# A token sum moved from ones-matmuls on TensorE to accumulating DMAs in float32

## Chip, cores, metric

One core of one Trainium2 chip. The metric is the device time of one launch in microseconds (us); lower is better.

## The reference, cut to what matters

The program mixes a linear-attention block and an MLP-like block over 2048 tokens of 640 features. Only this part of the attention block matters here:

```python
phi = lambda t: jnp.where(t > 0, t + 1, jnp.exp(t)) + 1e-6
pq, pk = phi(q), phi(k)
kv = jnp.einsum("bhsd,bhse->bhde", pk, v)
z = jnp.einsum("bhsd->bhd", pk)                     # sum of phi(k) over the 2048 tokens
num = jnp.einsum("bhqd,bhde->bhqe", pq, kv)
den = jnp.einsum("bhqd,bhd->bhq", pq, z)[..., None] + 1e-6
o = num / den
```

The change is about how `z`, a vector of 640 sums, is made. It is needed for `den` alone.

## The kernel before

The kernel is a fixed sequence of instructions on each engine (it schedules by hand). In SBUF, tokens lie on 128 partitions in 16 chunks; `pk` is `[128, 16, 640]` in bfloat16. The stages that matter, in order on TensorE: the K stage (to about 32 us) makes `pk`; the Q stage (32 to 74 us) is ten groups, each of ten Q matmuls and five steps of G = x^T pk; then come the `w1_unit`s, with `den_unit`, `kv_unit` and others put between them.

```python
def z_rows():                      # 32 matmuls; sums each 4th chunk into one of 4 column tiles
    p = alloc()
    for (n0, n1) in COLS:          # (0, 512), (512, 640)
        for cc in range(0, NCH, 4):
            for q in range(4):
                mm(PP[p][32 * q:32 * (q + 1), n0:n1], lhsT=ones32[:], rhs=pk[:, cc + q, n0:n1],
                   start=(cc == 0), stop=(cc == NCH - 4), tile_position=(0, 32 * q), ...)
    act(zsb[:], PP[p][:, 0:D], ACT.Copy)
    release(p)
    nc.vector.tensor_copy(zhi[:], zsb[:])
    nc.vector.tensor_tensor(zlo[:], zsb[:], zhi[:], op=ALU.subtract)

def z_cols():                      # 10 matmuls of one column: puts z on partitions
    ...
    for j in range(DC):
        mm(PP[p][:, j:j + 1], lhsT=zh[:, j], rhs=c32[:], start=True, stop=False)
        mm(PP[p][:, j:j + 1], lhsT=zl[:, j], rhs=c32[:], start=False, stop=True)
    nc.vector.tensor_copy(zT[:], PP[p][:, 0:DC])
    for j in range(DC):
        nc.vector.tensor_scalar(Zb[:, j, :], mask32, zT[:, j:j + 1], None, op0=ALU.mult)

# Q stage, ten groups (n_ = 0..9)
    ... # ten Q matmuls, phi, ln1_s (squares on ACT, every 4th also rs1 on POOL), ln1_a (lnxs on DVE,
        # then a transposing DMA lnxT<-lnxs), five g_unit steps
    if n_ == 2:
        z_rows()
    if n_ == 4:
        z_cols()
...
w1_unit(0, 4)        # its gelu goes to shs; then 4 copies of shs on DVE
den_unit()           # needs Zb
rec_piece(0)
w1_unit(0, 0)
kv_unit()
...
```

POOL (GpSimd) computes `rs1`, the layernorm scale of four chunks at a time. `zhi` is z rounded to bfloat16, `zlo` the rest; z_cols multiplies both.

## Time and profile before

| | before |
|---|---|
| time, median of 4 runs | 267.95 us (267.28 to 268.35) |
| span of the profiled run | 266.3 us |
| TensorE (PE) busy | 259.6 us, 97% |
| share of PE in the chain that ended last | 95% |
| z_rows on PE, start to start of the next group | 1.21 us |

The page of the kernel before, its busy times and the engines of the chain that ended last (PEld is the loading of weights into TensorE, DVE is VectorE, ACT ScalarE, POOL GpSimd, SP SyncE; a q marks an engine's sequencer):

```profile
PE 259.6 (97%) x1666; PEld 136.1 (51%) x1699; DVE 116.0 (44%) x212; ACT 110.7 (42%) x165; POOL 32.9 (12%) x111
...
PE 95%; DMA 2%; issue 1%; DVE 0%; SPq 0%
```

PE is busy nearly all the time, and the chain of waits runs through it. Only removing PE time, or making PE wait, can change the total.

The timeline of PE before. Columns: start us, length us, engine, line of the kernel, operation, out<-in, shape, count. L364 is z_rows, L390 the Q matmuls, L423 a w1_unit, L470 den_unit, L443 kv_unit:

```profile
42.99 1.27 PE L364 MATMUL pp<-RPK,ones 128*32 128x512 bf16 x32
44.20 2.35 PE L390 MATMUL pp<-RXT,RA 128*128 128x512 bf16 x9
...
73.59 2.32 PE L423 MATMUL pp<-lnxT,w1x 128*128 128x512 bf16 x10
75.84 1.26 PE L470 MATMUL pp<-pqT,Zb 128*32 128x512 bf16 x20
77.04 2.33 PE L423 MATMUL pp<-lnxT,RB 128*128 128x512 bf16 x9
79.21 1.76 PE L443 MATMUL pp<-RB,RA 128*120 128x120 bf16 x30
```

Read the starts, not the lengths: the 32 matmuls of z_rows run four at a time on column tiles, and from 42.99 to 44.20 they cost 1.21 us. That is the most that removing them can give. PE passes from one stage to the next without a gap.

POOL before, the end of the rs1 work of chunks 4 to 7; the changed kernel starts its DMAs behind it:

```profile
40.61 1.18 POOL L222 TENSOR_TENSOR rs<-ve,nhalf 128x4 f32<-128x4 f32 x1
```

### The profile page before, as it was taken

How to read it: one execution, taken by the hardware profiler on the slowest of the kernel's cores; microseconds unless marked ns; L12 is line 12 of the kernel's file. 1: busy time of each engine (PE TensorE's matmuls, PEld its weight loads, DVE VectorE, ACT ScalarE, POOL GpSimd, SP SyncE). 2: the span in 40 equal slices, each digit the busy share in tenths (PEclk: the TensorE clock that was granted, in tenths of full speed). 3: DMA queues.
4: the chain of work that ended last, by engine and by line, in shares of the span. 5: the costliest groups of instructions: out<-in, count | busy, mean ns of one | idle time of the engine just before them, and what ended most of it. 6: DMA issues, size and time to landing. Idle time of an engine off the chain costs nothing.

```text
span 266.3 us, 4195 instructions
## 1 busy us (share of the span) xinstructions
PE 259.6 (97%) x1666; PEld 136.1 (51%) x1699; DVE 116.0 (44%) x212; ACT 110.7 (42%) x165; POOL 32.9 (12%) x111
## 2 busy tenths in 40 slices
PE   7999999999999999999999999999999999999995
PEld 3555555555545445554444455555544444555552
DVE  2486748665655065999930033233200002233232
ACT  3466663665355771244977522022034444022020
POOL 5000132020200000536870000000000000000000
PEclk9999999999999999999999999999999999999999
DMA  6999993431340269932652001001000000001001
GB/s 204 169 192 301 365 225 68 62 75 25 77 98 0 59 213 362 313 83 49 101 100 49 0 2 49 27 25 49 27 25 0 2 0 0 25 27 49 27 25 49
DMA packets 42245, 23.95 MB, mean 90 GB/s; under 512 B 31090, under 2 KB 41458, under 8 KB 42226
## 3 DMA queue, kind: packets, MB, share of 16 engines
q1 hardware_dynamic: 41474, 22.99, 36.1%
q10 hardware_dynamic: 720, 0.69, 0.8%
q8 instruction: 13, 0.21, 0.3%
q14 instruction: 6, 0.05, 0.1%
q0 software_dynamic: 32, 0.00, 0.0%
HBM read 12.86 MB, written 3.44 MB: 61 GB/s over the span
## 4 chain that ended last, share of the span: by engine, by line
PE 95%; DMA 2%; issue 1%; DVE 0%; SPq 0%
PE pp L638 20%; PE pp L571 19%; PE pp L423 8%; PE pp L597 8%; PE pp L390 8%; PE pp L556 8%; PE pp L261 8%; PE pp L252 8%; DMA RXH<-in_A_x_dram 2%; PE pp L580 2%; PE pp L623 1%; PE pp L632 1%; PE pp L587 1%; PE pp L457 1%; PE pp L443 1%
## 5 line engine op out<-in xcount | busy, mean ns | idle before, releaser
L638 PE MATMUL pp<-RB,RXH 128*128 128x128 bf16 (+1 forms) x381 | 53.5, 297 | 0.7 <-issue 0.3
L571 PE MATMUL pp<-lnxT,RA 128*128 128x512 bf16 x235 | 51.9, 379 | 0.3
L638 PEld LDWEIGHTS <-RXH 128*128 128x128 bf16 x390 | 29.7, 98 | 24.2 <-issue 2.1
L571 PEld LDWEIGHTS <-RA 128*128 128x128 bf16 x240 | 23.4, 98 | 28.0
L600 ACT ACTIVATE RXH<-pp,g_all 128x640 f32<-128x640 f32 x16 | 12.7, 794 | 54.9 <-PE pp L597 54.9
L573 ACT ACTIVATE RXH<-pp 128x1024 bf16<-128x1024 f32 x24 | 24.2, 1019 | 26.7 <-PE pp L571 26.7
L244 ACT ACTIVATE eb<-pp 128x640 bf16<-128x640 f32 (+1 forms) x26 | 21.4, 828 | 25.2 <-PE pp L390 16.3
L261 PE MATMUL pp<-RPK,RXH 128*128 128x128 bf16 (+1 forms) x157 | 25.0, 297 | 0.2
L252 PE MATMUL pp<-RA,RXT 128*128 128x512 bf16 (+1 forms) x157 | 24.0, 300 | 0.2
L390 PE MATMUL pp<-RXT,RA 128*128 128x512 bf16 x97 | 23.1, 379 | 0.2
L597 PE MATMUL pp<-Mp,pqT 128*128 128x512 bf16 (+1 forms) x158 | 23.0, 298 | 0.1
L602 DVE SCALAR_TENSOR_TENSOR RPK<-RPK,omg,RXH 128x640 f32<-128x640 f32 x8 | 7.1, 885 | 36.5 <-ACT RXH L600 36.5
L556 PE MATMUL pp<-w,RXH 128*128 128x128 bf16 (+1 forms) x157 | 21.7, 297 | 0.2
L423 PE MATMUL pp<-lnxT,RB 128*128 128x512 bf16 x77 | 18.1, 379 | 0.2
L261 PEld LDWEIGHTS <-RXH 128*128 128x128 bf16 x160 | 12.7, 98 | 10.4
L247 DVE TENSOR_SCALAR eb<-eb 128x640 bf16<-128x640 bf16 (+1 forms) x26 | 9.5, 365 | 19.3 <-ACT eb L244 19.3
L602 DVE SCALAR_TENSOR_TENSOR RXT<-RXT,omg,RXH 128x640 f32<-128x640 f32 x8 | 7.1, 884 | 24.6 <-ACT RXH L600 24.6
L252 PEld LDWEIGHTS <-RXT 128*128 128x128 bf16 x160 | 12.6, 98 | 9.5 <-DVE RA L329 0.2
L597 PEld LDWEIGHTS <-pqT 128*128 128x128 bf16 x160 | 12.2, 98 | 10.0 <-issue 0.8
L556 PEld LDWEIGHTS <-RXH 128*128 128x128 bf16 x160 | 12.3, 98 | 9.6
L607 DVE SCALAR_TENSOR_TENSOR RXH<-pp,omg,RXT 128x640 bf16<-128x640 f32 x8 | 7.1, 884 | 19.8 <-PE pp L638 19.8
L390 PEld LDWEIGHTS <-RA 128*128 128x128 bf16 x100 | 11.1, 118 | 8.9
(110 smaller groups left out, 238.4 us busy)
## 6 DMA issues: line engine op xcount, KB each, us to landing
out_dram<-RXH SPq DMA_DIRECT2D x15, 160.0 KB, 1.8
RA<-in_B_w_dram SPq DMA_DIRECT2D x5, 432.0 KB, 6.9
RA<-in_A_wqkv_dram SPq DMA_DIRECT2D x2, 800.0 KB, 8.9
RB<-in_B_w_dram SPq DMA_DIRECT2D x1, 1120.0 KB
RXH<-in_A_x_dram SPq DMA_DIRECT2D x2, 480.0 KB, 4.7
RB<-in_B_w_dram SPq DMA_DIRECT2D x1, 960.0 KB, 13.6
RB<-in_B_w_dram SPq DMA_DIRECT2D x1, 800.0 KB, 8.5
Mp<-Mscr SPq DMA_DIRECT2D x1, 800.0 KB
```

Source lines behind the costliest of these rows:

```text
L244: act(e[:, 0:n], src, ACT.Exp)
L252: mm(PP[p][:, n0:n1], lhsT=xT[:, dc, c * P:(c + 1) * P], rhs=wkg[:, dc, n0:n1], start=(dc == 0), stop=(dc == DC - 1))
L261: mm(PP[p][:, n0:n1], lhsT=x_sb[:, c, i * P:(i + 1) * P], rhs=pk[:, c, n0:n1], start=(c == 0), stop=(c == NCH - 1))
L390: mm(PP[p][:, tt * 512:(tt + 1) * 512], lhsT=wqp[:, dc, j], rhs=xT[:, dc, t0:t0 + 512], start=(dc == 0), stop=(dc == DC - 1))
L423: mm(PP[p][:, tt * 512:(tt + 1) * 512], lhsT=lh, rhs=lnxT[:, dc, t0:t0 + 512], start=(dc == 0), stop=(dc == DC - 1))
L556: mm(PP[p][:, n0:n1], lhsT=hsT[:, fc, 2 + c * P:2 + (c + 1) * P], rhs=w2[:, fc, n0:n1], start=(fc == 0), stop=(fc == DC - 1))
L571: mm(PP[p][:, k * 512:(k + 1) * 512], lhsT=w3[:, dc, (fc + k) * P:(fc + k + 1) * P], rhs=lnxT[:, dc, t * 512:(t + 1) * 512], start=(dc == ...
L573: act(h2T[:, t % 2, fc:fc + 2, :], PP[p][:].rearrange("p (k s) -> p k s", k=2), ACT.Gelu_apprx_tanh)
L597: mm(PP[p][:, n0:n1], lhsT=pqT[:, j, c * P:(c + 1) * P], rhs=Mp[:, j, n0:n1], start=(j == 0), stop=(j == DC - 1))
L600: act(ga, PP[p][:, 0:D], ACT.Copy, scale=g_all[:, c:c + 1])
L602: nc.vector.scalar_tensor_tensor(x1(c), x1(c), omg[:, c:c + 1], ga, op0=ALU.mult, op1=ALU.add)
L638: mm(PP[p][:, n0:n1], lhsT=h2T[:, k, fc, cc], rhs=w4[:, fc, n0:n1], start=False, stop=(fc == NF - 1))
```

## The change

The intent: take the 32 ones-matmuls off the busiest engine. Eight DMAs, issued from POOL during the Q stage, add `pk` into a float32 accumulator of `[128, 1280]`, two chunks each; the DMA engines do the adding. Below, one such DMA is a link of the chain, and its landing is the moment when its completion is signalled. TensorE only turns the remaining 128 token rows onto partitions (`z_cols`), now behind `w1_unit(0, 4)`.

```diff
+    RMP = sb("RMP", DC * D)
+    Mp = RMP[:].rearrange("p (j d) -> p j d", j=DC)
+    zacc = RMP[:, 0:4 * D].bitcast(F32)
...
-    def z_rows():            (whole function)
+    def z_add(k):
+        nc.gpsimd.dma_start(zacc, RPK[:, 2 * k * D:2 * (k + 1) * D],
+                            **({"accum_op": ALU.add} if k else {}))
+
+    def z_sum():
+        nc.vector.tensor_tensor(zsb[:], zacc[:, 0:D], zacc[:, D:2 * D], op=ALU.add)
         nc.vector.tensor_copy(zhi[:], zsb[:])
         nc.vector.tensor_tensor(zlo[:], zsb[:], zhi[:], op=ALU.subtract)
...
-            if n_ == 2:
-                z_rows()
-            if n_ == 4:
-                z_cols()
+            if 1 <= n_ <= 8:
+                z_add(n_ - 1)
...
     pop(ln1_a, 4)
+    z_sum()
...
     w1_unit(0, 4)
+    z_cols()                 (its constant c32, 1/32, is now onec, 1)
+    w1_unit(0, 0)
     den_unit()
     rec_piece(0)
-    w1_unit(0, 0)
```

All eight DMAs write the same bytes, so each is issued only after the completion of the one before. The Trainium skill, "DMA: Bandwidth & Descriptors", section "Rules for kernel authors", says why this must be: an accumulating DMA reads its destination and writes it later, and nothing holds the bytes between.

More of the change, by code (lines that the diff above doesn't have):

```diff
@@ L86 @@
     w2 = sb("w2", DC * D)[:].rearrange("p (j d) -> p j d", j=DC)
-    Mp = sb("Mp", DC * D)[:].rearrange("p (j d) -> p j d", j=DC)
+    RMP = sb("RMP", DC * D)
+    Mp = RMP[:].rearrange("p (j d) -> p j d", j=DC)
+    zacc = RMP[:, 0:4 * D].bitcast(F32)
     pqT = sb("pqT", DC * S)[:].rearrange("p (j s) -> p j s", j=DC)
@@ L103 @@
     ident = sb("ident", P)
-    ones32 = sb("ones32", 32)
-    c32 = sb("c32", 1)
+    onec = sb("onec", 1)
     mask4 = sb("mask4", P)
@@ L181 @@
         nc.gpsimd.memset(wkg[:, dc, D + 1:D + 2], 1.0)
-    nc.gpsimd.memset(ones32[:], 1.0)
-    nc.gpsimd.memset(c32[:], 1.0 / 32)
+    nc.gpsimd.memset(onec[:], 1.0)
     nc.gpsimd.memset(nhalf[:], -0.5)
@@ L357 @@
     wqp = wq.rearrange("p k (q j) -> p k j q", j=DC)
-    def z_rows():
-        p = alloc()
-        for (n0, n1) in COLS:
-            for cc in range(0, NCH, 4):
-                for q in range(4):
-                    mm(PP[p][32 * q:32 * (q + 1), n0:n1], lhsT=ones32[:], rhs=pk[:, cc + q, n0:n1],
-                       start=(cc == 0), stop=(cc == NCH - 4), tile_position=(0, 32 * q), skip_group_check=True)
-        act(zsb[:], PP[p][:, 0:D], ACT.Copy)
-        release(p)
+    def z_add(k):
[3 more added lines that the diff above has]
+        nc.vector.tensor_tensor(zsb[:], zacc[:, 0:D], zacc[:, D:2 * D], op=ALU.add)
         nc.vector.tensor_copy(zhi[:], zsb[:])
@@ L375, in z_cols @@
         for j in range(DC):
-            mm(PP[p][:, j:j + 1], lhsT=zh[:, j], rhs=c32[:], start=True, stop=False)
-            mm(PP[p][:, j:j + 1], lhsT=zl[:, j], rhs=c32[:], start=False, stop=True)
+            mm(PP[p][:, j:j + 1], lhsT=zh[:, j], rhs=onec[:], start=True, stop=False)
+            mm(PP[p][:, j:j + 1], lhsT=zl[:, j], rhs=onec[:], start=False, stop=True)
         nc.vector.tensor_copy(zT[:], PP[p][:, 0:DC])
@@ L495 @@
     w1_unit(0, 4)
+    z_cols()
+    w1_unit(0, 0)
     den_unit()
     rec_piece(0)
-    w1_unit(0, 0)
     kv_unit()
```

## The prediction

> **What bounds the kernel now.** TensorE does. The page gives PE 97% busy of 266.3 us, the chain of waits is 95% PE. DVE (44%), ACT (42%) and POOL (12%) have slack. Only PE time removed or PE waits added can move the total.
>
> **What the change removes from PE.** In the timeline, the 32 ones-matmuls of z_rows start at 42.99 us and the next Q group starts at 44.20: four column tiles run together, so they cost 1.21 us, not their summed busy time. The ten z_cols matmuls stay (51.26 to 51.65, 0.39 us), but move behind w1_unit(0,4). The possible gain is 1.2 us, 0.45%. DVE gains an f32 add (about 0.82 us, as the zlo subtraction).
>
> **What it adds.** Eight DMAs issued from POOL, each reading 128x1280 bf16 (328 KB) and writing 128x1280 f32 (655 KB); seven also read the 655 KB back to add. All hit the same bytes, so each one waits for its predecessor's completion: a serial chain. The first is behind the rs1 work of chunks 4 to 7, which ends at 41.8 us on POOL.
>
> Cost of one link: the only POOL-issued DMA in this trace (gate_w, 1.2 KB) held POOL 0.81 us and landed 3.5 us after issue, though at the busy start. The Trainium skill, "DMA: Bandwidth & Descriptors", section "Anatomy of one DMA", fits 2.0 us plus bytes/436 GB/s for this path[...]. With 983 KB read by an accumulating link this gives 4.3 us, plus about 0.8 us of issue: estimate 5.2 us, plausibly 4 to 7. No run shows it yet.
>
> **Critical path.** With 1.6 us taken out before it, w1_unit(0,4) would end at 75.84 - 1.6 = 74.2 us, and z_cols wants zhi and zlo then. z_sum needs 2.1 us of DVE (add 0.82, cast 0.49, subtraction 0.82). So the eighth DMA must land by about 72.1: (72.1 - 41.7)/8 = 3.8 us per link is the break-even. At 5.2 us it lands at 83.3, z_cols starts at about 85.5, and PE stands idle about 11 us. No later PE slack absorbs that. At start, matmuls of 512 columns took 607 to 634 ns against 379 later. The Trainium skill, "TensorE: Matmul & The Clock Gate", Part 1, says that the clock halves after some 3.4 us of idleness; then the restart costs some 1.5 us more.
>
> Even with no DMA wait, DVE now does the four shs copies (1.72 us, starting 1.16 us after w1_unit(0,4) ends) before the zT copy and Zb; den_unit after w1_unit(0,0) would wait about 1 us. So the best case is close to a tie, 267 to 268.
>
> **Sum.** 267.8 - 1.2 + 11.3 + about 1.5 (clock) + 0.5 (Zb behind the shs copies) = about 280; I take 279 for the chance of shorter links.
>
> **What would show it.** The eight issues start about 5.2 us apart from 41.7 us; the wait view shows DVE waiting for the last accumulating DMA at the z_sum add and PE waiting at the first zhi weight load; long 512-column matmuls follow the gap.
>
> **What would make it wrong.** Links under 4 us (then 267 to 269: no gain, because of the Zb wait); slower adds in the DMA engines, or transposes and DVE work delaying them (7 us: 293 or more).
>
> Chances: faster by over 2% 0.01, within 2% 0.29, slower by over 2% 0.70. Predicted 279, range 267.5 to 293.

## More of the kernel before

DVE before, where it waits for the rs1 of chunks 12 to 15 (in brackets the idle time and what ended it):

```profile
71.54 1.16 DVE L226 TENSOR_SCALAR lnxs<-RXH,me,rs 128x640 bf16<-128x640 bf16 x3 [0.64 <-POOL rs L222]
```

## The result

| | before | after |
|---|---|---|
| median of 4 runs | 267.95 us | 280.88 us (280.28 to 282.67) |
| ratio of fast runs, 95% interval | 1 | 1.0496 (1.044 to 1.0552) |
| span of the profiled run | 266.3 us | 281.0 us |
| mean granted TensorE clock (1 is full speed) | 0.999 | 0.975 |

Ratios in this document are the mean time of one kernel's fast runs over the mean of the other's of the same rounds, so not quite the ratio of the medians quoted. The change made the kernel 5% slower.

The page of the kernel after, the lines that answer to those of before, and its DMA issues (KB of one, median us from issue to landing):

```profile
PE 262.4 (93%) x1667; PEld 135.4 (48%) x1667; DVE 116.7 (42%) x213; ACT 110.1 (39%) x164; POOL 40.3 (14%) x118
...
PE 88%; DMA 7%; DVE 2%; issue 1%; POOL 1%; ACT 0%; POOLq 0%
...
RMP<-RPK POOLq DMA_DIRECT2D x8, 640.0 KB, 4.5
```

DMA has entered the chain. PE after, same columns; in brackets the idle time before an instruction and what ended it. L420 is a w1_unit, L373 and L374 are z_cols, L467 is den_unit, L440 kv_unit:

```profile
71.87 2.32 PE L420 MATMUL pp<-lnxT,w1x 128*128 128x512 bf16 x10
86.78 0.20 PE L373 MATMUL pp<-onec,zhi 128*128 128x1 bf16 x1 [12.59 <-DVE zhi L365]
87.64 0.20 PE L374 MATMUL pp<-onec,zlo 128*128 128x1 bf16 x1 [0.66 <-DVE zlo L366]
...
88.02 4.43 PE L420 MATMUL pp<-lnxT,RB 128*128 128x512 bf16 x10
92.38 1.52 PE L467 MATMUL pp<-pqT,Zb 128*32 128x512 bf16 x20
93.83 1.81 PE L440 MATMUL pp<-RB,RA 128*120 128x120 bf16 x30
```

w1_unit(0, 4) starts 1.72 us earlier than before (71.87 against 73.59), as promised. Then PE stands idle for `zhi`, again for `zlo`, and the next stage of the same ten matmuls takes 4.43 us in place of 2.33. From kv_unit to the end both kernels need the same: 266.3 - 79.21 = 187.1 us before, 281.0 - 93.83 = 187.2 us after. So the whole loss lies between 71.9 and 93.8 us.

POOL after, the eight issues of the DMAs (L360) and one line of the rs1 work:

```profile
41.61 0.69 POOL L360 DMA_DIRECT2D RMP<-RPK  x1
46.68 0.91 POOL L360 DMA_DIRECT2D RMP<-RPK  x1 [4.37 <-DMA RMP<-RPK]
52.83 1.04 POOL L360 DMA_DIRECT2D RMP<-RPK  x1 [5.24 <-DVE lnxs L226]
59.72 0.85 POOL L360 DMA_DIRECT2D RMP<-RPK  x1 [5.85 <-DMA RMP<-RPK]
...
64.63 0.93 POOL L360 DMA_DIRECT2D RMP<-RPK  x1 [1.77 <-DVE eb L247]
70.92 0.88 POOL L360 DMA_DIRECT2D RMP<-RPK  x1 [5.36 <-DMA RMP<-RPK]
75.85 0.86 POOL L360 DMA_DIRECT2D RMP<-RPK  x1 [4.06 <-DMA RMP<-RPK]
80.80 0.86 POOL L360 DMA_DIRECT2D RMP<-RPK  x1 [4.09 <-DMA RMP<-RPK]
...
82.87 1.04 POOL L222 TENSOR_TENSOR rs<-ve,nhalf 128x4 f32<-128x4 f32 x1
```

The issues come 4.9 to 6.9 us apart, 5.6 on average ((80.80 - 41.61)/7). Two of the waits are put down to DVE, but only in name: each of those issues too started about 0.5 us after the DMA before it had landed, like the rest. DVE after, the end of the wait for z:

```profile
83.94 1.51 DVE L226 TENSOR_SCALAR lnxs<-RXH,me,rs 128x640 bf16<-128x640 bf16 x4 [14.77 <-POOL rs L222]
85.37 0.82 DVE L364 TENSOR_TENSOR zsb<-RMP 128x640 f32<-128x640 f32 x1
86.23 0.49 DVE L365 CAST zhi<-zsb 128x640 bf16<-128x640 f32 x1
86.75 0.83 DVE L366 TENSOR_TENSOR zlo<-zsb,zhi 128x640 bf16<-128x640 f32 x1
```

Here a surprise: DVE waited 14.77 us not for the last DMA but for `rs1` of POOL, which stood behind the eighth issue in POOL's order. The DMA issued at 80.80 landed 4.4 us later, at 85.2, just before DVE gets to the `zsb` add (85.37). Two waits end at nearly the same time; the profile names one. Which of them costs the 13 us can only be told by taking each away. That is what the first experiments do.

The sum of the loss in the profiled runs, from the starts above (a w1_unit takes 2.17 us from its start to the next, so the first of them ends at 74.04):

| part | us |
|---|---|
| w1_unit(0, 4) starts earlier | -1.72 |
| w1_unit(0, 4) itself, 2.17 against 2.25 from start to start | -0.08 |
| z_cols, its ten matmuls once zlo is there (87.64 to 88.02) | +0.38 |
| PE idle for zhi (74.04 to 86.78) | +12.74 |
| PE from the first zhi matmul to zlo (86.78 to 87.64) | +0.86 |
| w1_unit(0, 0) slower: 4.36 against 2.17 | +2.19 |
| den_unit slower: 1.45 against 1.20 | +0.25 |
| sum | +14.62 |

The spans differ by 281.0 - 266.3 = 14.7 us; the small rest lies after the start of kv_unit. That is more than the 12.9 us between the medians, because the profiled run of the changed kernel, 282.67 us, was the slowest of its four (the profiled run before took 268.0 us).

### The profile page after: what moved, and what is told of

Read it like the earlier page. It is cut to its first block, busy times and chain, and to the rows that moved or that the text cites. A ratio compares the mean times of both kernels' runs of the same rounds, so it can differ in the third digit from the quotient of the medians.

```text
span 281.0 us, 4188 instructions
## 1 busy us (share of the span) xinstructions
PE 262.4 (93%) x1667; PEld 135.4 (48%) x1667; DVE 116.7 (42%) x213; ACT 110.1 (39%) x164; POOL 40.3 (14%) x118
## 3 DMA queue, kind: packets, MB, share of 16 engines
q1 hardware_dynamic: 41474, 22.99, 33.4%
q0 software_dynamic: 1184, 5.24, 7.4%
## 4 chain that ended last, share of the span: by engine, by line
PE 88%; DMA 7%; DVE 2%; issue 1%; POOL 1%; ACT 0%; POOLq 0%
PE pp L636 19%; PE pp L569 18%; PE pp L252 8%; PE pp L595 8%; PE pp L420 8%; PE pp L554 8%; PE pp L387 7%; PE pp L261 5%; DMA RMP<-RPK 5%; DMA g<-in_gate_w_dram 2%; PE pp L578 2%; PE pp L621 1%; PE pp L630 1%; PE pp L585 1%; PE pp L454 1%
## 5 line engine op out<-in xcount | busy, mean ns | idle before, releaser
L636 PE MATMUL pp<-RB,RXH 128*128 128x512 bf16 (+1 forms) x390 | 54.4, 299 | 0.0
L571 ACT ACTIVATE RXH<-pp 128x1024 bf16<-128x1024 f32 x24 | 24.3, 1021 | 26.7 <-PE pp L569 26.7
L261 PE MATMUL pp<-RPK,RXH 128*128 128x512 bf16 (+1 forms) x160 | 25.2, 299 | 0.0
L595 PE MATMUL pp<-RMP,pqT 128*128 128x512 bf16 (+1 forms) x160 | 23.1, 299 | 0.0
L554 PE MATMUL pp<-w,RXH 128*128 128x512 bf16 (+1 forms) x160 | 21.9, 299 | 0.0
L420 PE MATMUL pp<-lnxT,RB 128*128 128x512 bf16 x80 | 20.4, 411 | 0.0
L425 ACT ACTIVATE RXH<-pp 128x1024 bf16<-128x1024 f32 x8 | 8.2, 1028 | 25.8 <-PE pp L420 25.8
```

Of the source, the lines that this page charges most:

```text
L261: mm(PP[p][:, n0:n1], lhsT=x_sb[:, c, i * P:(i + 1) * P], rhs=pk[:, c, n0:n1], start=(c == 0), stop=(c == NCH - 1))
L420: mm(PP[p][:, tt * 512:(tt + 1) * 512], lhsT=lh, rhs=lnxT[:, dc, t0:t0 + 512], start=(dc == 0), stop=(dc == DC - 1))
L554: mm(PP[p][:, n0:n1], lhsT=hsT[:, fc, 2 + c * P:2 + (c + 1) * P], rhs=w2[:, fc, n0:n1], start=(fc == 0), stop=(fc == DC - 1))
L571: act(h2T[:, t % 2, fc:fc + 2, :], PP[p][:].rearrange("p (k s) -> p k s", k=2), ACT.Gelu_apprx_tanh)
L595: mm(PP[p][:, n0:n1], lhsT=pqT[:, j, c * P:(c + 1) * P], rhs=Mp[:, j, n0:n1], start=(j == 0), stop=(j == DC - 1))
L636: mm(PP[p][:, n0:n1], lhsT=h2T[:, k, fc, cc], rhs=w4[:, fc, n0:n1], start=False, stop=(fc == NF - 1))
```

## The experiments

The theory: the eight dependent DMAs form a chain whose end sets when z is ready, and PE waits for it. Rivals: the new place of z_cols costs; POOL's in-order queue (rs1 behind the DMAs) costs; the traffic of the DMAs slows everything; the long matmuls after the gap have another cause than the clock. "Wrong on purpose" marks kernels that do not compute the reference's sum. Every other kernel was correct; of the marked ones, e6_half_links counts half of the tokens twice.

### e1_order_only: z_cols moved, no DMA

```diff
 before
-            if n_ == 4:
-                z_cols()
     w1_unit(0, 4)
-    den_unit()
-    rec_piece(0)
+    z_cols()
     w1_unit(0, 0)
+    den_unit()
+    rec_piece(0)
```

> The kernel before with z_cols alone moved behind w1_unit(0,4); the sum is still made by z_rows on TensorE. No accumulating DMA. Theory (a serial chain of DMAs is the loss): about 0.5 to 1.0 us slower than before (268.4 to 269.0), because the first Zb now stands behind the four shs copies on DVE and den_unit waits for it about 0.7 us; no gap at z_cols. Rival (the new place of z_cols is the loss): near 280.

Measured: 268.70 us against 268.10 before; ratio 1.0012 (0.9982 to 1.0041). The gap at z_cols is absent, and den_unit waits 0.80 us for Zb, which stands behind the four shs copies on DVE. In the run times this is within noise. The new place is not the loss.

### e3, e4, e5: which of the two waits?

e3 takes rs1 out from behind the DMAs. e4 takes away the add's dependence on the DMAs. e5 does both. All eight DMAs run in all three.

```diff
 e3_rs1_first, against after
-            if 1 <= n_ <= 8:
+            if 1 <= n_ <= 5:
                 z_add(n_ - 1)
+            if n_ == 9:                 # behind the rs1 of chunks 12 to 15
+                for k in (5, 6, 7):
+                    z_add(k)
 e4_sum_no_dma, against after (wrong on purpose)
-        nc.vector.tensor_tensor(zsb[:], zacc[:, 0:D], zacc[:, D:2 * D], op=ALU.add)
+        zfk = pqT[:, 0, 0:2 * D].bitcast(F32)
+        nc.vector.tensor_tensor(zsb[:], zfk, zfk, op=ALU.add)
 e5_both_off (wrong on purpose): both edits
```

> The changed kernel with links 5, 6 and 7 issued after the rs1 work of chunks 12 to 15 on POOL, so that the layernorm never waits behind a DMA. Chain theory: the last link lands at the same time (about 85.3 us in the trace), so 280.9 stays within 0.5 us, and DVE now shows a wait for the DMA at the zsb add. Rival (POOL's in-order queue holds back rs1, and with it DVE; the chain view of the changed kernel goes through rs1): the gap closes, about 268.

> Wrong result on purpose: the zsb add reads pqT in place of the accumulator, all eight links still run. If only the DMA wait at the add counted, about 268. If, as I think, the late rs1 alone holds DVE to the same time (it ended at 83.9 us, the add began at 85.4), still about 280.5 to 281.

> Wrong result on purpose: both edits of the two runs before. All eight links run with their bytes and contention, but nothing on DVE or TensorE waits for them. Chain theory: the gap is gone, 267.2 to 268.2: 1.2 us less from z_rows, about 0.7 to 1.0 us more from Zb behind the shs copies. Rival (the traffic itself slows transposes or other engines): clearly above 269.

| kernel | rs1 behind DMAs | add waits for DMAs | median us | ratio to before (95%) |
|---|---|---|---|---|
| e3_rs1_first | no | yes | 283.11 | 1.0542 (1.0503 to 1.0582) |
| e4_sum_no_dma | yes | no | 281.36 | 1.0482 (1.0445 to 1.052) |
| e5_both_off | no | no | 267.31 | 0.9966 (0.9933 to 1.0) |

The kernel before took 268.10 us in the same rounds. DVE in e4_sum_no_dma, still held by rs1:

```profile
82.54 1.51 DVE L226 TENSOR_SCALAR lnxs<-RXH,me,rs 128x640 bf16<-128x640 bf16 x4 [13.78 <-POOL rs L222]
```

DVE in e3_rs1_first:

```profile
86.14 0.83 DVE L364 TENSOR_TENSOR zsb<-RMP 128x640 f32<-128x640 f32 x1 [14.75 <-DMA RMP<-RPK]
```

With rs1 out of the way, the wait shows under its own name, and it is no shorter. Either wait alone is enough for the whole loss; only both removed close the gap. Both come from the same chain: rs1 is late because the seven DMAs before the eighth issue are. From the eighth issue to the start of the zsb add it was 4.57 us after the change (85.37 - 80.80), the same in e4_sum_no_dma (83.97 - 79.40), and 4.39 in e3_rs1_first (86.14 - 81.75): in the changed kernel the way over rs1 was the longer one, by some 0.2 us, with the landing close behind. The rival that blames POOL's order alone falls, and so does the one that blames traffic: e5_both_off moves the same bytes and is no slower than before. Its PE, at the place of the gap:

```profile
74.37 0.18 PE L375 MATMUL pp<-onec,zlo 128*128 128x1 bf16 x1
74.41 2.32 PE L424 MATMUL pp<-lnxT,RB 128*128 128x512 bf16 x10
77.53 1.26 PE L471 MATMUL pp<-pqT,Zb 128*32 128x512 bf16 x20 [0.80 <-DVE Zb L379]
```

Of the 1.2 us gained by dropping z_rows, the 0.80 us wait for Zb takes back most. e3_rs1_first missed its number by 2 us (283.11 against an expected 280.9 within 0.5); e4_sum_no_dma came 0.4 us above its range. Its issues show why: with rs1 early, the transposing DMAs of chunks 12 to 15 run beside the sixth and seventh DMA, whose issue-to-next-issue times became 6.26 and 5.66 us, against 4.93 and 4.95 after the change, where those transposes came late.

### e9_filler: is it the clock?

```diff
 after
     w1_unit(0, 4)
+    p = alloc()
+    for _ in range(56):
+        mm(PP[p][:, 0:512], lhsT=warm[:, 0:P], rhs=warm[:], start=True, stop=True)
+    release(p)
     z_cols()
```

> The changed kernel with 56 matmuls of 512 columns on zeros (about 12.1 us) between w1_unit(0,4) and z_cols, in the gap. Theory of the clock: the array stays at full clock, w1_unit(0,0) takes 2.3 us in place of 4.4 and den_unit 1.26 in place of 1.52, but then den_unit waits some tenths for Zb; about 1.5 to 2.3 us faster than the changed kernel, so 278.6 to 279.4. Rival (those matmuls were long for another reason, such as DMA traffic at their operands): unchanged, 280.9.

Measured: 279.61 us, ratio to before 1.043 (1.0377 to 1.0484). The median is just outside what I expected, and 1.3 us below the changed kernel of another session; the intervals of the two ratios overlap. The trace is clearer. The three stretches of the kernel after are the gap, the rest of z_cols, and w1_unit(0, 0) with den_unit; behind the engines' busy times comes the granted clock:

```profile
74.15:86.78 12.63, 0.04 (x2) 0.01 (x1) 2.77 (x7) 1.05 (x2) 3.64 (x7) 0.70 0.53 130
86.78:88.02 1.24, 0.58 (x11) 0.50 (x12) 1.17 (x4) 0.00 (x0) 0.00 (x0) 0.50 0.67 132
88.02:93.83 5.81, 5.81 (x35) 1.83 (x33) 2.67 (x11) 1.03 (x1) 0.00 (x0) 0.58 0.43 59
```

And PE of e9_filler in the same place:

```profile
87.47 0.20 PE L374 MATMUL pp<-onec,zlo 128*128 128x1 bf16 x1 [0.66 <-DVE zlo L366]
...
87.85 2.32 PE L420 MATMUL pp<-lnxT,RB 128*128 128x512 bf16 x10
90.14 1.26 PE L467 MATMUL pp<-pqT,Zb 128*32 128x512 bf16 x20
91.33 1.81 PE L440 MATMUL pp<-RB,RA 128*120 128x120 bf16 x30
```

With the array kept busy, the ten matmuls take 2.32 us again and den_unit 1.26. From the zlo matmul to kv_unit PE needs 91.33 - 87.47 = 3.86 us, against 93.83 - 87.64 = 6.19 us: the clock costs 2.3 us. The rival (DMA traffic at the operands) falls, for the DMAs are the same. This agrees with the Trainium skill, "TensorE: Matmul & The Clock Gate", Part 1, by which the clock halves after idleness: the granted clock was 0.50 between 86.78 and 88.02, and 1.00 in e9_filler from 87.85 to 91.33.

### e6_half_links and e8_plain_links: what a link is made of

```diff
 e6_half_links (wrong on purpose): one chunk a link
-        nc.gpsimd.dma_start(zacc, RPK[:, 2 * k * D:2 * (k + 1) * D],
+        nc.gpsimd.dma_start(zacc[:, 0:D], RPK[:, 2 * k * D:(2 * k + 1) * D],
 ... (z_sum adds zacc[:, 0:D] to itself)
 e8_plain_links (wrong on purpose): overwrite, no adding
-                            **({"accum_op": ALU.add} if k else {}))
+                            **{})
```

> Wrong result on purpose: each link takes only one chunk (640 elements a partition), half the bytes, the chain still of eight. Measures fixed cost against bytes. If a link of 4.45 us to landing is about 2.3 fixed and 2.2 of data, it lands in about 3.3 us, the chain ends near 41.6 + 8 x 4.0 = 74 us and the total is 269 to 272. If fixed cost is nearly all, landing stays at 4.2 or more.

> Wrong result on purpose: the eight links overwrite in place of adding, so the accumulator is not read back; source bytes, written bytes and the chain are the same. Measures the price of the read-back. If the 655 KB read back cost what the prediction's estimate gave them (983 KB against 655 KB, 0.75 us a link), a link lands in about 3.7 us alone and the total falls to about 272 to 275. If the read-back hides behind the write, landing stays at 4.4 and the total near 281.

Landing of the DMAs after issue, from the views of the accumulator's tile (min, median, max) of the kernel after, of e6_half_links and of e8_plain_links:

```profile
DMA to landing us min/median/max: 4.4/4.5/6.4
```

```profile
DMA to landing us min/median/max: 3.3/3.8/4.3
```

```profile
DMA to landing us min/median/max: 3.3/3.6/4.8
```

Half the bytes save 1.1 us of the minimum. If time is linear in bytes, a full link has 2.2 us of data and 2.2 us fixed; this is an estimate from those two minima. Without the read-back, a link of full width saves 1.1 us too, 0.3 us of it in the issue itself, which held POOL 0.54 us in place of 0.87 (medians). The totals were 274.2 and 272.56 us: e6 missed its 269 to 272, since its median link (3.8 us) was longer than the 3.3 I had used; e8 came out as expected if the read-back costs. The prediction had 4.3 us for a link, from the skill's fit and the 983 KB read, and 0.8 us of issue on top. Measured from the start of the issue, and so with the issue in it, the best links took 4.4 us, and the next issue started some 0.5 us after the landing: 4.9 against 5.2. The sum is near, but its parts are not quite those of the prediction: the issue is inside the 4.4, and the 0.5 us was not in it.

### e2_two_chains and e7_four_wide: shorten the chain, keep the bytes

```diff
 e2_two_chains: even links into zacc, odd links into zaccB (free columns of hsT)
+    o_ = NCH * D + S + 4
+    zaccB = RXH[:, o_:o_ + 2 * (S + 4)].bitcast(F32).rearrange("p (c s) -> p c s", c=2)[:, :, 2:2 + D]
-        nc.gpsimd.dma_start(zacc, RPK[:, 2 * k * D:2 * (k + 1) * D],
-                            **({"accum_op": ALU.add} if k else {}))
+        nc.gpsimd.dma_start(zaccB if k % 2 else zacc, pk[:, 2 * k:2 * k + 2, :],
+                            **({"accum_op": ALU.add} if k > 1 else {}))
 ... (z_sum: two more adds)
 e7_four_wide: four links of four chunks, accumulator [128, 4, 640] in hsT
-        nc.gpsimd.dma_start(zacc, RPK[:, 2 * k * D:2 * (k + 1) * D],
+        nc.gpsimd.dma_start(zacc, pk[:, 4 * k:4 * k + 4, :],
-            if 1 <= n_ <= 8:
+            if 1 <= n_ <= 4:
 ... (z_sum: two more adds)
```

> Even links into one accumulator, odd links into a second one (free columns of hsT), so two links are in flight; the same bytes, two more adds on DVE (1.7 us). Chain theory: POOL waits for the link before last, so eight links take about four to five link times plus some contention, the last lands near 41.6 + 28 = 70 us, z_cols waits little or not: 267.3 to 270. Rival (bytes or the DMA engines bind, not the wait of each link): the last still lands after 80 us, 277 to 281.

> Four links of four chunks each into one accumulator of four rows of 640 float32 (columns of hsT); the same bytes read and written, half the dependent steps. If a link is about 2.5 us fixed and 2 us of data, a wide one takes about 7 us and the chain ends near 41.6 + 28 = 70 us: 267.3 to 270. If the bytes set the time (4.5 us of data in a link of 5), a wide link takes about 9.5 us and the result stays near 278 to 281.

Measured: e2 273.85 us, ratio 1.0227 (1.0172 to 1.0282); e7 281.55 us, ratio 1.0501 (1.0449 to 1.0553). Both numbers missed the theory's. For e2, the direction is right: more than half of the loss is gone though two adds of 0.83 us were added. The last accumulating DMA landed at 72.9 us, some 3 us later than expected. But what holds DVE now is a third thing:

```profile
73.44 0.45 DVE L228 TENSOR_SCALAR lnxs<-RXH,me,rs 128x640 bf16<-128x640 bf16 x1 [2.74 <-DMA lnxT<-lnxs]
74.11 0.45 DVE L228 TENSOR_SCALAR lnxs<-RXH,me,rs 128x640 bf16<-128x640 bf16 x1 [0.23 <-DMA lnxT<-lnxs]
74.47 0.82 DVE L366 TENSOR_TENSOR zsb<-RMP 128x640 f32<-128x640 f32 x1
```

`lnxs` waits for its buffer, which a transposing DMA must empty first, and these DMAs were slower beside the accumulating ones. Their median from issue to landing, from 38 to 95 us, is 5.0 us in e2, against 2.6 us before and 3.5 us after the change; the accumulating DMAs themselves took 5.4 and 7.7 us (medians of the two chains). So what is in flight beside a link matters: I had counted the wait of each link and not the company. How much of the 7.7 us is company stays open, for the second accumulator lies in rows that are not contiguous, and the queue of the accumulating DMAs moved the same 5.24 MB in 1664 packets, against 1152 after the change. In e7 it was 2112, so a wide link is not simply two links either. It took 8.4 us to landing (median), not 7. The chain did become shorter: its last link, issued at 69.58, landed 8.5 us later at 78.1 us, against 85.2 after the change. The trace puts down what was lost again to POOL's order: rs1 of chunks 8 to 11 stands behind the last issue and ended at 73.1 us. No run takes this wait away in e7. DVE in e7_four_wide:

```profile
73.12 0.80 DVE L227 TENSOR_SCALAR lnxs<-RXH,me,rs 128x640 bf16<-128x640 bf16 x2 [11.48 <-POOL rs L223]
```

DVE idled 11.48 us inside the Q stage for it, and PE then 4.11 us. So neither the number of steps nor the end of the chain alone gives the time; what stands behind an issue in its engine's order counts as well.

### e10_two_early: two chains, started one group earlier

```diff
 against e2_two_chains
-            if 1 <= n_ <= 8:
-                z_add(n_ - 1)
+            for k in {0: (0, 1), 1: (2, 3), 2: (4,), 3: (5,), 4: (6, 7)}.get(n_, ()):
+                z_add(k)
 ... (and z_cols with Zb ahead of the shs copies of w1_unit(0, 4))
```

> Two accumulators as in e2_two_chains, the first two links one Q group earlier (about 35.5 us), none held behind rs1 work, and Zb ahead of the shs copies on DVE. If the chain's end and the Zb wait are the only losses, the last link lands near 62 us, z_cols and den_unit wait for nothing, and the 1.2 us of z_rows appear: 266.5 to 267.2, against 267.9 before. If contention with the transposes of lnx still holds DVE past 72 us: 268 to 271.

Measured: 273.53 us, ratio 1.0208 (1.0185 to 1.0231): outside both ranges, and no better than e2. The first odd link, issued at 36.20, landed 9.25 us later by the chain of waits (the late weight loads were still running; in the changed kernel the DMA engines are 93% busy from 32 to 41.6 us), and the next two took 8.11 and 8.13. The eighth issue came at 63.37, rs1 of chunks 8 to 11 behind it, and DVE idled 4.43 us for it. Starting earlier only moved the DMAs into busier DMA engines.

### e11_pool_adds: POOL adds itself

```diff
 against after
-        nc.gpsimd.dma_start(zacc, RPK[:, 2 * k * D:2 * (k + 1) * D],
-                            **({"accum_op": ALU.add} if k else {}))
+        nc.gpsimd.tensor_tensor(zacc, zacc if k > 1 else RPK[:, 0:2 * D],
+                                RPK[:, 2 * k * D:2 * (k + 1) * D], op=ALU.add)
 ... (seven adds at n_ = 0..4; z_sum at n_ = 5, z_cols at n_ = 7)
```

> The same float32 sum made by seven adds of 128x1280 on POOL itself in place of the DMAs, z_sum and z_cols inside the Q stage as before. If an add takes about 2 us and does not hold up DVE much, nothing waits: 266.5 to 267.2. If POOL's adds and DVE's two-operand work exclude each other (port sharing), phi is late and the Q stage stretches: 268 or more, with long DVE instructions in the trace.

Measured: 271.36 us, ratio 1.0144 (1.0124 to 1.0165). DVE and PE in e11_pool_adds, two views:

```profile
45.25 4.11 DVE L226 TENSOR_SCALAR lnxs<-RXH,me,rs 128x640 bf16<-128x640 bf16 x2
49.28 2.87 DVE L247 TENSOR_SCALAR eb<-eb 128x1024 bf16<-128x1024 bf16 x1
```

```profile
53.53 4.00 PE L387 MATMUL pp<-RXT,RA 128*128 128x512 bf16 x10 [3.17 <-DVE pqT L248]
```

Two lnxs take 0.79 us in the kernel before, and the eb instruction 0.43 us; here they take 4.11 and 2.87 us beside POOL adds of about 2.7 us each. The Trainium skill, "SBUF — State Buffer", section "Who interferes with whom", states that tensor_scalar on DVE can enter a mode which shares a port pair with GpSimd, and that the later of the two then waits for the whole instruction. The trace agrees with that: the pair of lnxs is 3.3 us longer and the eb 2.4 us, about the length of a POOL add. I had expected the two-operand work of DVE to suffer; the pqT instructions kept their 1.22 us. PE then waits 3.17 us inside the Q stage, and its clock drops as well (ten matmuls in 4.00 us, granted clock 0.56 from 53.53 to 57.37).

### e12_late_use: keep the DMAs, need z later

```diff
 against e3_rs1_first
-    z_sum()                       (before w1_unit(0, 4))
-    z_cols()
-    den_unit()                    and rec_piece(0..3) between the units
     w1_unit(0, 4) ... w1_unit(0, 3)
+    z_sum()
     ...
     w1_unit(1, 4)                 # with z_cols and Zb ahead of its shs copies
     w1_unit(1, 0)
+    den_unit(); rec_piece(0..3)
     w1_unit(1, 1); w1_unit(1, 2); w1_unit(1, 3)
+    rexp_unit()
-    scale_q(0..4, 0)              (all ten now in the w3 stage)
```

> The changed kernel with its eight serial links as they are (rs1 of chunks 12 to 15 ahead of links 5 to 7, as in e3_rs1_first), but everything that needs z moved later: z_sum after w1_unit(0,3), z_cols and Zb at w1_unit(1,4), den_unit after w1_unit(1,0), the reciprocals and rexp behind it, all scale_q in the w3 stage. Chain theory: the sum is ready on TensorE's side near 88.4 us, about when w1_unit(1,4) ends (88.5), so TensorE waits for nothing and the 1.2 us of z_rows appear: 266.4 to 267.4 against 267.9 before (ratio 0.994 to 0.998). If the DMAs cost something else than the wait, or the reordering makes new waits: 268 or more.

Measured: 267.90 us against 267.84 before; ratio 0.9998 (0.997 to 1.0027); my 266.4 to 267.4 is missed. The chain is as long as ever (the eighth issue at 83.84 us), and the kernel is no slower than before:

```profile
89.65 0.20 PE L373 MATMUL pp<-onec,zhi 128*128 128x1 bf16 x1
90.50 0.20 PE L374 MATMUL pp<-onec,zlo 128*128 128x1 bf16 x1 [0.66 <-DVE zlo L366]
```

The wait for zhi is gone from this view; 0.66 us for zlo remain, and they take back half of what dropping z_rows gave. From the first Q matmul to the end, the profiled runs need 267.1 - 33.4 = 233.7 us, against 266.3 - 32.1 = 234.2 before: 0.5 us better, smaller than the noise of the run times. That profiled run reached its first Q matmul 1.3 us later than the kernel before, and its six runs spread from 266.52 to 269.35 us; I do not know whether this is chance. No version tried is faster than before beyond its interval.

## Why the prediction was right

Predicted 279 us (range 267.5 to 293), measured 280.88. Point by point, with the numbers of the profiled runs:

- **What bounds the kernel; gain at most 1.2 us.** Right. w1_unit(0, 4) starts 1.72 us earlier, of which z_cols gives back 0.38.
- **A serial chain of about 5.2 us a link.** Right in kind; the mean distance between issues was 5.6 us. Links without company took 4.9 us, those beside the transposes of lnx 6 to 7 us (the first link, which only copies, 5.1 us beside them). The prediction named those transposes as a risk and gave them no time.
- **PE idle about 11 us.** It was 12.74 us for zhi and 0.86 to zlo, 13.6 in all: the term (11.3 in the sum) was undersized by 2.3 us in the profiled run, most of which the last link's later end (85.2 against 83.3 us) explains.
- **The clock, 1.5 us.** Right in kind, undersized: 2.44 us by the table, and 2.3 us by e9_filler.
- **Zb behind the shs copies, 0.5 us.** It did not show after the change: in the gap the gelu had long been done, so DVE began the shs copies at 88.07 us, as soon as it was free. In e9_filler, with a fast w1_unit(0, 0), PE shows no wait for Zb either. It is real where there is no gap: 0.80 us in e1_order_only and e5_both_off.
- **What would show it.** One sign was wrong: DVE was to be seen waiting for the last DMA at the zsb add, and it was seen waiting for rs1 on POOL. The prediction had not put rs1 of chunks 12 to 15 behind the eighth issue on DVE's path to z. e3, e4 and e5 showed that both waits were there and that each alone costs the whole. That the way over rs1, which the prediction did not see, ends within some 0.2 us of the one that it did see is luck.

The sum: -1.2 + 11.3 + 1.5 + 0.5 = 12.1 us was predicted in place of -1.34 + 13.6 + 2.44 + 0 = 14.7 in the profiled runs (less the 0.08 of the table), and 280.88 - 267.95 = 12.9 us in the medians. The closeness of the medians to the prediction is thus better than that of its terms in the profiled run.

## What to carry to other kernels

Work taken from the busiest engine is free only if its result still comes before that engine asks for it: count dependent steps times the latency of one, and compare with the time there is (here eight times 4.9 us or more, against 30). When two waits end together, the profile names one; take each away alone and both together before you believe it. A chain that can't be made short can be made harmless by using its result later (e12_late_use), but then ask whether the gain, 1.2 us of 268, was worth it.

## What the Trainium skill lacked or had wrong

- "DMA: Bandwidth & Descriptors", "Anatomy of one DMA": the fit of 2.0 us plus bytes/436 GB/s does not say which bytes count for an accumulating DMA. Here a link reading 983 KB and writing 655 KB landed 4.4 us after the start of its issue at best, near the 4.3 that the bytes read give; without the read-back of 655 KB it landed after 3.3 us, where the fit gives 2.8 by the bytes read and 3.5 by the bytes written (estimates from the fit).
- The same page, "Issuing engines are not separate DMA queues", says that DMAs interleave, but not how much small transposes suffer: the lnx transposes went from a median of 2.6 us to 3.5 us in the changed kernel (one accumulating DMA at a time) and 5.0 us in e2_two_chains (two), and the accumulating DMAs from 4.5 us to 5.4 and 7.7 us (the latter in more packets as well).
- "TensorE: Matmul & The Clock Gate", Part 1, gives a window of about 3.4 us for both ways, free-running, and so no length for a slow stretch. Here, after the change, the granted clock was 1.00 for 5.1 us more after PE fell idle (74.19 to 79.29) and 0.50 until 92.94, 5.3 us after the first zlo matmul (87.64), so all ten matmuls of w1_unit(0, 0) and a part of den_unit ran slow; a gap shown as 3.17 us (e11_pool_adds) was enough for ten slow matmuls (4.00 us in place of 2.32).
- No page draws out, as a cost to plan for, that a DMA issue waiting in GpSimd's queue holds back unrelated GpSimd work (the premises, order within a queue and the wait at the issuing engine, do stand there): here rs1 ended at 83.9 us, and that alone cost the whole 13 us (e4_sum_no_dma).
